# Products of constant ones in TensorE's waits, in a kernel of two attention layers and two Fourier layers

## The chip, the cores and the metric

The kernel runs on one core of one Trainium2 chip. The metric is the device time of that core in microseconds (us), lower is better. A core has TensorE (PE: matrix products into PSUM), VectorE (DVE), ScalarE (ACT) and GpSimd (POOL), and SyncE (SP), whose queue issues the transfers (DMA). Each engine works through its own list of instructions in order; an instruction waits until the semaphores that it names have the counts it asks for.

## The reference

Four sublayers are applied to x (2048 rows of 512 values), each on a layer norm of x and added to x:

```
x = x + A(layernorm(x)); x = x + B(layernorm(x)); x = x + A(layernorm(x)); x = x + B(layernorm(x))

A: q, k, v = x@wq, x@wk, x@wv in 32 heads of 16, four segments of 512 rows
   for each segment: p = softmax(q k^T / 4 + causal mask); a_dot = p v
      a_mem = phi(q) M / (phi(q) z + 1e-6);  o = g a_mem + (1 - g) a_dot
      M += phi(k)^T v;  z += sum phi(k)
   out = o @ wo
B: a = x @ dft_hid_re^T;  b = x @ dft_hid_im^T;  y = dft_seq_re @ a - dft_seq_im @ b
```

## The kernel before, in words

**Products.** Most products of float32 operands are made from float16 pairs (a high and a low half): three products of 128x128 by 128x512 for each block of 128 in the sum (`mm3`, lines 348 to 350). So TensorE's usual instruction is a weight load (LDWEIGHTS) of 128x128 and a product with 512 columns. The scores of the attention are products of 48 or 50 rows, two at a time on the two halves of the rows; the products with v have 32 output rows.

**Generators.** Each part of the work is a generator: `s_p` makes q and k of a segment and of a group of eight heads, `s_x` the scores whose row maxima VectorE takes, `s_st` the transposed scores whose exponentials ScalarE takes, `s_av` the products with v, `s_o` the output projection, `s_ab` and `s_f` the two transforms of B, and `t_...` the steps of other engines that follow a product. A generator yields what its next step needs: the engine, the tiles it reads, and the buffers it will take (`need`, lines 335 and 336).

**PSUM.** The eight banks of PSUM are the tiles `b`, one pool that `take` and `close` hand out by kind: `pj`, `av`, `dft`, `sx`, `st`, `ss`. A product in a bank must wait until the engine that read the bank's last contents is done.

**Where things stand in time.** Up to some 200 us the inputs and weights are loaded and split, and the first segment's attention runs alone. After that the Fourier products of B fill TensorE between the attention's steps, and from some 1480 us on little but Fourier products is left.

## Time and profile before

| | |
|---|---|
| three runs | 1747.06, 1746.74, 1741.66 us; median 1746.74 |
| the profiled execution | 1747.35 us, of which 1745.6 us is the span from the first to the last instruction |
| mean clock granted to TensorE | 0.971 of full speed |
| busy share | PE 96%, DVE 63%, ACT 50%, POOL 43% |

The profile gives for each group of instructions when it began, how long it took, what it wrote and read, how many there were (x), and in brackets how long its engine had been idle just before, with what ended the idle time. A product's record is longer (381 ns in the mean for 128x512) than the step from one start to the next, since a product begins while the last one drains; so a busy TensorE in the page is not one at its peak. "PEclk" is the clock that was granted to TensorE, 1.00 or 0.50 in one slice, as a mean over the stretch.

### The profile page before, as it was taken

How to read it: one execution, taken by the hardware profiler on the slowest of the kernel's cores; microseconds unless marked ns; L12 is line 12 of the kernel's file. 1: busy time of each engine (PE TensorE's matmuls, PEld its weight loads, DVE VectorE, ACT ScalarE, POOL GpSimd, SP SyncE). 2: the span in 40 equal slices, each digit the busy share in tenths (PEclk: the TensorE clock that was granted, in tenths of full speed). 3: DMA queues.
4: the chain of work that ended last, by engine and by line, in shares of the span. 5: the costliest groups of instructions: out<-in, count | busy, mean ns of one | idle time of the engine just before them, and what ended most of it. 6: DMA issues, size and time to landing. Idle time of an engine off the chain costs nothing.

```text
span 1745.6 us, 32094 instructions
## 1 busy us (share of the span) xinstructions
PE 1674.4 (96%) x10998; PEld 730.6 (42%) x10998; DVE 1094.4 (63%) x3525; ACT 870.9 (50%) x1481; POOL 746.2 (43%) x1284
## 2 busy tenths in 40 slices
PE   6888899998999999999999999999999999999999
PEld 3333344443344443444535344443444443344444
DVE  7885856787675967654578676566675856443221
ACT  5597467555548365644366755464446334412000
POOL 4466355555546264633244644444535334312000
PEclk9788999999999999999989999999999999999999
DMA  8537445554247443334845654354444342131423
GB/s 194 165 102 205 109 113 156 150 145 128 77 125 212 139 130 107 108 105 135 223 139 189 188 164 121 74 138 132 113 120 122 94 110 85 56 121 23 136 85 118
DMA packets 217076, 225.00 MB, mean 129 GB/s; under 512 B 112968, under 2 KB 135496, under 8 KB 216912
## 3 DMA queue, kind: packets, MB, share of 16 engines
q1 hardware_dynamic: 216912, 222.95, 45.6%
q8 instruction: 86, 1.41, 0.3%
q14 instruction: 78, 0.64, 0.1%
HBM read 137.40 MB, written 61.87 MB: 114 GB/s over the span
## 4 chain that ended last, share of the span: by engine, by line
PE 80%; DVE 7%; issue 4%; DMA 3%; ACT 3%; POOL 2%; SPq 1%; DVEq 0%; POOLq 0%; ACTq 0%
PE b L258 80%; DVE junk L258 3%; ACT w L258 3%; POOL w L258 2%; DMA w<-w 1%; SPq L258 1%; DVE w L258 1%; DVE y L258 1%; DVE mx L258 1%; DMA x<-y 0%; DMA w<-in_x_dram 0%; DMA y<-in_wv_dram 0%; DVE bst L258 0%; DMA w<-x 0%; DVE cgm L258 0%
## 5 line engine op out<-in xcount | busy, mean ns | idle before, releaser
L258 PEld LDWEIGHTS <-w 128*128 128x128 f16 x4992 | 466.2, 98 | 636.9 <-issue 121.5
L258 PE MATMUL b<-w,w 128*128 128x512 f16 x3072 | 709.9, 381 | 4.2 <-POOL w L258 1.4
L258 ACT ACTIVATE w<-b,fac 128x512 f32<-128x512 f32 (+1 forms) x728 | 417.6, 653 | 196.1 <-PE b L258 191.8
L258 DVE CUSTOM_DVE_ANT_0 junk<-b,cmask 128x128 bf16<-128x128 f32 (+3 forms) x1024 | 437.1, 485 | 70.9 <-PE b L258 70.1
L258 POOL TENSOR_TENSOR w<-w,w 128x512 f16<-128x512 f32 (+1 forms) x260 | 309.2, 1193 | 239.1 <-ACT w L258 204.7
L258 POOL TENSOR_SCALAR_AFFINE_SELECT w<-w 128x128 f32<-128x128 f32 (+2 forms) x704 | 236.7, 348 | 272.6 <-ACT w L258 268.1
L258 DVE SCALAR_TENSOR_TENSOR y<-b,fyu,y 128x512 f32<-128x512 f32 x200 | 149.1, 745 | 210.7 <-PE b L258 209.8
L258 PE MATMUL b<-g,w 128*128 128x512 f16 x768 | 191.1, 394 | 6.7 <-POOL w L258 3.0
L258 ACT ACTIVATE w<-w,csc 128x512 f16<-128x512 f32 (+1 forms) x256 | 179.5, 721 | 25.2 <-DVE csc L258 20.3
L258 PE MATMUL b<-w,vt 128*32 128x512 f32 (+3 forms) x2048 | 181.5, 469 | 6.9 <-POOL w L258 4.7
L258 PE MATMUL b<-wd,w 128*128 128x512 f16 x768 | 182.1, 385 | 4.6 <-DMA w<-w 4.3
L258 ACT ACTIVATE w<-b 128x512 f16<-128x512 f32 x128 | 76.4, 599 | 218.0 <-PE b L258 210.6
L258 DVE SCALAR_TENSOR_TENSOR w<-b,w 128x512 f16<-128x512 f32 x128 | 87.9, 688 | 150.2 <-ACT w L258 149.2
L258 PE MATMUL b<-kst,qst 48*128 48x128 f16 (+3 forms) x1024 | 125.0, 309 | 10.9 <-DVE mx L258 5.0
L258 PE MATMUL b<-qst,kst 50*128 50x512 f16 (+3 forms) x1024 | 119.5, 308 | 10.4 <-DVE mx L258 3.8
L258 ACT ACTIVATE w<-w 128x512 f16<-128x512 f32 (+1 forms) x144 | 90.6, 632 | 58.1 <-DVE w L258 55.9
L258 PEld LDWEIGHTS b<-w,vt 128*32 128x32 f32 x2048 | 56.7, 113 | 95.8 <-issue 52.2
L258 PE MATMUL b<-w,g 128*128 128x128 f16 x1536 | 94.4, 219 | 0.4 <-ACT w L258 0.2
L258 PEld LDWEIGHTS <-g 128*128 128x128 f16 x1536 | 87.8, 98 | 13.9 <-issue 9.1
L258 DVE STREAM_TRANSPOSE w<-b 128x512 f32<-128x512 f32 x112 | 76.4, 699 | 22.1 <-PE b L258 13.7
L258 PE MATMUL b<-wo,w 128*128 128x512 f16 x384 | 89.3, 381 | 0.0
L258 PEld LDWEIGHTS <-kst 50*128 50x128 f16 x1024 | 37.5, 95 | 120.8 <-issue 109.5
(99 smaller groups left out, 1017.8 us busy)
## 6 DMA issues: line engine op xcount, KB each, us to landing
w<-in_cs_dram SPq DMA_DIRECT2D x128, 256.0 KB, 3.6
cc<-w SPq DMA_DIRECT2D x128, 256.0 KB, 2.5
w<-cc SPq DMA_DIRECT2D x128, 256.0 KB, 3.3
w<-w SPq DMA_DIRECT2D x96, 256.0 KB, 3.2
d<-w SPq DMA_DIRECT2D x128, 128.0 KB, 2.5
w<-in_x_dram SPq DMA_DIRECT2D x32, 256.0 KB, 3.2
qst<-d SPq DMA_DIRECT2D x64, 128.0 KB, 3.2
kst<-d SPq DMA_DIRECT2D x64, 128.0 KB, 2.8
```

The source lines that it names most:

```text
L258: r = f(*args, **kw)
```

## The change

Before TensorE's next step is taken, a new function `t_warm` looks at the planned time `at` at which that step can begin, less 200 ns. If TensorE would be idle for at least 220 ns until then, if the products of the last 3413 ns by the plan have under 6500 columns, and if a bank of PSUM of kind `dft` is free at least 430 ns before, then products of the constant tile `onesb` (128x128 ones in bfloat16, there before) with itself, repeated to 512 columns, go to TensorE into that bank, each counted as 215 ns, until the time is up or 6500 columns are reached. Nobody reads the bank's contents. They bypass `Plan.op`, and the books on the bank are put back, so that the plan doesn't see them, and the next step that takes a bank takes that one. Two lines in `op` and the helper `lately` keep the list of columns that the function looks at.

```diff
+WARM, IDLE, SPARE = 6500, 220.0, 200.0
...
+    def lately(self, t):
+
+        return sum(c * max(0.0, min(e, t) - max(b, t - TICK)) / (e - b) for b, e, c in self.work)
...
             self.cols[int((t + c) / TICK)] = self.cols.get(int((t + c) / TICK), 0) + cols
+            self.work.append((t, t + c, cols))
+            while self.work[0][1] < t - 3 * TICK:
+                self.work.popleft()
...
+    def t_warm(at):
+        now, at = pl.free["T"], at - SPARE
+        if "CM" not in done or at - now < IDLE or pl.lately(at) >= WARM:
+            return
+        r = pl.slots_free(("dft",))
+        if r is None or r > at - 430:
+            return
+        now = max(now, r)
...
+        p = ps("dft")
+        while now + 215 < at and pl.lately(at) < WARM:
+            T.real.matmul(p, onesb, onesb.unsqueeze(1).to_broadcast([128, 4, 128]), start=True, stop=True)
+            pl.work.append((now, now + 215, 512))
+            now += 215
...
+        if best[1][0][0] == "T":
+            t_warm(best[0])
         best[1][0] = next(best[1][1], None)
```

The lists of DVE, ACT, POOL and SP are the same as before. TensorE's list has the same instructions in the same order, and 241 products of ones (each with its weight load) between them, in 39 groups. By the place in the profile of before at which the next instruction begins (us), with the number of products:

| Place | Products put in ahead of it |
|---|---|
| 9.47, 15.34, 16.55 | 37, 23, 4 |
| 47.50 to 51.19 | 1, 4, 2, 4, 8, 13 |
| 76.9 and 154.5 | 1 and 2 |
| 113.1 to 134.0 | 2, 2, 3, 3, 4 |
| 140.22 to 143.32 | 15, 7, 5, 1 |
| 185.75, 185.91, 190.56 | 16, 12, 18 |
| 409.4 to 434.8 | 3, 2, 2, 1, 2 |
| 518.9 and 560.06 | 1 and 6 |
| 684.56, 822.46, 838.32 | 4, 14, 3 |
| 890.2 to 891.6 | 2, 4, 2 |
| 976.2, 986.1, 1445.1 | 3, 2, 3 |

The first place is on PE at some 186 us, at the end of an output projection (`b<-wo,w` ends just ahead), where three pairs of scores (`kst,qst`: `qst` is loaded, `kst` streams) stand ahead of the first transform of B (`wd`). Before:

```order
L258 LDWEIGHTS qst_106
L258 MATMUL b_2791<-kst_104,qst_106 128x384
L258 LDWEIGHTS qst_106
L258 MATMUL b_2792<-kst_104,qst_106 128x384
L258 LDWEIGHTS qst_106
L258 MATMUL b_2801<-kst_104,qst_106 128x384
L258 LDWEIGHTS qst_106
L258 MATMUL b_2802<-kst_104,qst_106 128x384
L258 LDWEIGHTS w_2662
L258 MATMUL b_2811<-wd,w_2662 128x512
```

and in the changed kernel, where `L1180` is the line of the new products and L268 is the helper's line that was L258:

```order
L1180 LDWEIGHTS onesb
L1180 MATMUL b_2952<-onesb 128x512
...
L268 LDWEIGHTS qst_106
L268 MATMUL b_2969<-kst_104,qst_106 128x384
...
L1180 LDWEIGHTS onesb
L1180 MATMUL b_2979<-onesb 128x512
...
L268 LDWEIGHTS qst_106
L268 MATMUL b_2992<-kst_104,qst_106 128x384
...
L1180 MATMUL b_3002<-onesb 128x512
...
L268 MATMUL b_3021<-wd,w_2823 128x512
```

The second and the third pair of scores now stand behind 16 and 12 products of ones, and the transform behind 18 more.

The second place is on PE at 838 us, where the projection of a new segment (`g` holds the transposed, normed rows) follows the products of the Fourier transform along the rows (`b<-w,w`). Before:

```order
L258 MATMUL b_11034<-w_10449,w_10965 128x512
L258 LDWEIGHTS w_8329
L258 MATMUL b_11053<-g_10803,w_8329 128x512
L258 LDWEIGHTS w_8329
L258 MATMUL b_11053<-g_10803,w_8329 128x512
```

and in the changed kernel, with the semaphores that each waits for (DMAHW: transfers; PE: TensorE's own count):

```order
L268 MATMUL b_11288<-w_10688,w_11219 128x512
L1180 LDWEIGHTS onesb
L1180 MATMUL b_11307<-onesb 128x512
...
L268 LDWEIGHTS w_8563 [waits DMAHW5_49,DMAHW7_49,DMAHW3_49,DMAHW0_49]
L268 MATMUL b_11311<-g_11042,w_8563 128x512 [waits PE_49]
```

Three products of ones stand ahead of the weight load that waits for transfers, and the first product into the bank that held them names TensorE's own count: it waits until the last of them has ended. So it is behind every group whose bank the next step takes; ahead of the products with v (`w,vt`), which go on in a bank of their own, there is no such wait. In the whole list 139 rows wait for that count, 118 before.

## The prediction

> **What bounds the kernel now.** I read the page's slices and chain first.

> ```profile
> DVE  7885856787675967654578676566675856443221
> PEclk9788999999999999999989999999999999999999
> PE 80%; DVE 7%; issue 4%; DMA 3%; ACT 3%; POOL 2%; SPq 1%; DVEq 0%; POOLq 0%; ACTq 0%
> L258 PE MATMUL b<-w,w 128*128 128x512 f16 x3072 | 709.9, 381 | 4.2 <-POOL w L258 1.4
> ```

> TensorE carries 80% of the chain, so after the first 200 us what TensorE saves or loses moves the end one for one, while in slices two to four (44 to 175 us) the clock is lowest, and VectorE is busy to eight tenths in two of them. The clock is what the change works on. Its pieces, from the table by stretches (time, TensorE's busy time and records, clock):

> ```profile
> core 0: us, PE busy (x), PEclk, DMA share, GB/s
> 50.16:60.40 10.24, 6.73 (x26) 0.50 0.91 269
> 121.84:125.25 3.41, 3.16 (x15) 0.50 0.24 45
> 142.32:149.15 6.83, 6.13 (x20) 0.50 0.96 340
> 190.11:196.93 6.82, 6.37 (x16) 0.50 0.32 66
> 411.97:415.39 3.42, 3.42 (x21) 0.50 0.77 149
> 432.45:435.86 3.41, 2.17 (x20) 1.00 0.41 77
> 435.87:439.28 3.41, 3.27 (x10) 0.50 0.50 66
> 558.75:562.16 3.41, 1.89 (x19) 1.00 0.97 230
> 562.16:565.57 3.41, 2.80 (x15) 0.50 0.60 121
> 685.04:691.87 6.83, 6.63 (x26) 0.50 0.00 0
> 821.57:824.99 3.42, 1.29 (x6) 1.00 0.66 119
> 824.99:828.40 3.41, 3.41 (x10) 0.50 0.61 142
> 838.64:842.05 3.41, 3.41 (x10) 0.50 0.00 0
> 893.25:896.66 3.41, 3.41 (x20) 0.50 0.28 97
> 1658.32:1701.96 43.64, 43.64 (x204) 1.00 0.25 85
> ```

> The clock goes by slices of 3.41 us: a thin slice (821.57: six records; 558.75; 432.45) is followed by one at half speed. From the last row a product costs 43.64 / 204 = 0.214 us at full clock, so 16 fit in a slice, and twice that, 0.43, at half. A full slice at half clock loses 3.41 / 2 = 1.71 us of TensorE's work.

> The other side is where TensorE waits, from its timeline (start, time, instructions, idle just before):

> ```profile
> 9.47 0.59 PE L258 MATMUL b<-amax,ones 128*128 128x2 f32 x2 [9.47 <-DVE amax L258]
> 15.34 0.58 PE L258 MATMUL b<-amax,ones 128*128 128x2 f32 x2 [5.28 <-DVE amax L258]
> 16.55 4.81 PE L258 MATMUL b<-g,w 128*128 128x512 f16 x15 [0.63 <-DMA g<-w]
> 22.52 0.38 PE L258 MATMUL b<-amax,ones 128*128 128x1 f32 x2 [1.16 <-DVE amax L258]
> ...
> 47.50 2.88 PE L258 MATMUL b<-kst,qst 48*128 48x384 f16 x9
> ...
> 51.19 1.01 PE L258 MATMUL b<-g,w 128*128 128x512 f16 x2
> 55.22 0.61 PE L258 MATMUL b<-g,w 128*128 128x512 f16 x1 [3.01 <-POOL w L258]
> 56.10 0.40 PE L258 MATMUL b<-identf,mx 128*32 128x128 f32 x1 [0.28 <-DVE mx L258]
> ...
> 140.22 2.39 PE L258 MATMUL b<-qst,kst 50*128 50x512 f16 x8 [2.46 <-DMA qst<-mhl]
> 143.32 2.74 PE L258 MATMUL b<-g,w 128*128 128x512 f16 x6 [0.70 <-DMA w<-w]
> ...
> 185.57 0.66 PE L258 MATMUL b<-kst,qst 48*128 48x384 f16 x6
> 190.56 1.46 PE L258 MATMUL b<-wd,w 128*128 128x512 f16 x3 [4.32 <-DMA w<-w]
> ...
> 562.77 1.92 PE L258 MATMUL b<-w,vt 128*32 128x256 f32 x12 [2.09 <-POOL w L258]
> ...
> 822.46 0.61 PE L258 MATMUL b<-w,w 128*128 128x512 f16 x2 [0.75 <-ACT w L258]
> 824.45 11.79 PE L258 MATMUL b<-w,w 128*128 128x512 f16 x46 [1.38 <-POOL w L258]
> 838.32 4.45 PE L258 MATMUL b<-g,w 128*128 128x512 f16 x12 [2.08 <-DMA g<-w]
> ...
> 889.72 2.51 PE L258 MATMUL b<-kst,qst 48*128 48x384 f16 x8
> ...
> 1445.11 0.28 PE L258 MATMUL b<-identf,mx 128*32 128x128 f32 x1 [1.00 <-DVE mx L258]
> ```

> The products of ones were placed by planned waits. Some stand at a wait that the trace has (838.32, 1445.11), some a few products ahead of one (562.77), and some where there is none: the 16 and 12 within the six scores of 185.57.

> **What the products cost.** Nothing is removed or moved, no transfer and no queue of another engine is touched; so each group costs its number times 0.214 less what waits at or just behind it. By places:

> Start, 64 products, 13.7 us against 9.47 + 5.28 + 0.63 of waits. They can begin only when VectorE has written the ones:

> ```profile
> 1.50 0.17 DVE L258 MEMSET onesb<- 128x128 bf16 x1
> ```

> That is after 1.7 us, and the first run at half clock: ten at 0.43 and 27 at 0.214 end at 11.8, 2.3 late. VectorE's next maxima hang on that product, so the next two groups only follow, and the first projection begins at some 18.8 instead of 16.55, now at full clock: 15 x 0.214 = 3.2 against the 4.81 shown, so it ends at 22.0. The next product waits for VectorE until 22.52 anyway. Cost 0; if that cover fails, up to 1.

> 47 to 51 us, 32 products, 6.85. From 47.3 TensorE has some 2.1 us of its own work (twelve records, the scores in pairs, with the changes of shape) up to the product at 55.22: it gets there at 56.25, 1.03 late, of which the 0.28 ahead of 56.10 takes back some. Cost 0.75.

> 77 and 154 us: three products, 0.64. 113 to 134 us: 14 products; VectorE is busy in eight tenths of that slice and TensorE waits for it between the scores, so I count two as bare, 0.4.

> 137 to 143 us: 28 products, 6.0 us at full clock, less 2.46 and 0.70 of waits, and less some 1.1 that the eight scores save at full clock: 1.7 (they stood at half, 2.39).

> 185 to 190 us: 46 products, 9.84 less 4.32: 5.5, the largest item. The wait at 190.56 ends with a transfer that starts from work done before 185, so it doesn't move.

> 409 to 435 us: ten products among scores that wait for ScalarE's and VectorE's evictions; two bare, 0.4. 519 us: 0.2. 560 us: six, 1.28, within the 2.09 that ends at 562.77: 0. 684 us: four, 0.3 bare. 822 us: 14, 3.0 less 0.75 and 1.38: 0.9. 838 us: three, 0.64 under 2.08: 0. 890 us: eight at half clock, 3.4, less some 0.6 of pauses in the eight scores, whose row is all but busy: 2.8. 976 and 986 us: five bare, 1.1. 1445 us: 0.64 under 1.00: 0.

> Sum: 0.75 + 0.64 + 0.4 + 1.7 + 5.5 + 0.4 + 0.2 + 0.3 + 0.9 + 2.8 + 1.1 = 14.7 us.

> The wait for TensorE's own count is new. No row shows it alone. Its lower end is 0, where a wait follows anyway; its upper end is a product that can't begin while the last one drains, 0.381 - 0.214 = 0.17 us. Some 24 groups have no wait to hide it; at the middle, 0.1 (neither row is nearer), 2.4 us; at the upper end 4.1. **Cost: 17.1 us.**

> **What the clock gives back.** For each slice that the products fill, half the busy time of the slice that was at half speed behind it, where TensorE bounds:
> 50.16: from 56.1 to 60.4 only, 4.1 / 2 = 2.0. 121.84: 1.5. 142.32: its last 5.8 us, 2.9. 190.11: 3.2. 411.97: its second part alone, 1.3, as the first waits for ScalarE. 562.16: 1.4. 685.04: two slices, 3.3, but only the first products of that group fall into the slice before; even odds, 1.6. 824.99: 1.7. 838.64: 1.7. 893.25: 1.7. **Gain: 19.0 us.** The thin slices to which little or nothing is added stay (432.45 gets two products).

> Net: 17.1 - 19.0 = -1.9. The profiled execution took 1747.35, so 1745.4; that execution lies 0.6 above the median of the runs, so **1744.8 us**.

> [...] In the trace TensorE is idle for 1.24 us in all between 432.45 and 435.86 (3.41 less 2.17), and half clock follows. [...]

> **Rivals.** Within 0.3% is what a measurement of this kernel can't tell from no change (1741.5 to 1752.0); my forecast lies there, with a chance of 0.47 and that as its own range.

> Faster, 0.33: the own-count waits hide in the changes of shape (-2.4), the even-odds slices at 685 come back whole (+1.7), and the groups at 185 and 890 meet waits that the changed clock moves under them (some -3 of their 8.3). That is -1.9 - 2.4 - 1.7 - 3 = -9, 1738. For it: the slices after 200 us are full (3.41 of 3.41 busy), so nothing but TensorE can take their gain. Against it: the gains before 200 us (9.6) lie where VectorE is busy too.

> Slower, 0.13: the overrun decides. Its place is the six scores at 185.57 and the eight at 889.72, where the products stand ahead of work that doesn't wait, and the group at 137, which at half clock costs 28 x 0.43 = 12 instead of 6. If the clock isn't up by 137, the sum gets +6, and with a gain of 14.5 (the slices of 142 and 685 missed) it is 23.1 - 14.5 = +8.6: 1755. It decides once the gain is under 12 at the cost above.

> Slower, 0.05: only waits of a whole slice halve the clock, so that the ones between shorter waits buy nothing: 2.0 + 3.2 are won for 17.1, +11.9: 1758.6. Against it stand the rows of 432.45 and 558.75.

> Not what it says, 0.02: the clock doesn't count products that read the same constants; nothing is won, and what stands at half clock costs double (28 at 137, 46 at 185): 17.1 + 6.0 + some 8 = +31, 1778.

> **Chances and range.** Faster 0.33, within 0.47, slower 0.13 + 0.05 + 0.02 = 0.20. The range takes the faster case to 1736 (which leaves out some 0.06 below) and the slower ones to 1754 (0.13 above): 1736 to 1754.

> **What would show it.** In the changed profile: clock 1.00 in the stretches behind 56, at 143 to 149, 191 to 197, 562, 825 and 839 us, mean clock from 0.971 to some 0.985; the product at 55.22 about a microsecond late, the transform of 190.56 some 5 us later against the end of the output projection; no later start at 22.52 and behind 838. Half clock still there behind the filled slices refutes the gain; the transform on time at 190 refutes the largest cost; a 22.52 that moves shows that the start was not covered.

## The result, and the profile after

The changed kernel takes 1752.4 us, median of six runs (1749.98 to 1755.52), beside 1747.07 (1741.66 to 1748.81) for the kernel before: a ratio of 1.0036, interval 1.0018 to 1.0053. It is slower by 5.3 us where 2 us of gain were forecast. Run again beside the experiments it gave 1.0051 (1.0034 to 1.0068). Single runs of one kernel lie 10 us and more apart, so all comparisons below are of medians, with the 95% interval of the ratio to the kernel before.

The profiled execution took 1751.29 us, and its page shows a clock that rose and an end that came later all the same:

```profile
span 1749.6 us, 32573 instructions
PE 1707.0 (98%) x11239; PEld 746.3 (43%) x11239; DVE 1093.7 (63%) x3525; ACT 871.0 (50%) x1481; POOL 747.7 (43%) x1284
PEclk9889999999999999999989999999999999999999
PE 79%; DVE 8%; issue 4%; DMA 3%; ACT 3%; POOL 2%; SPq 1%; DVEq 0%; ACTq 0%; POOLq 0%
```

The mean clock is 0.985, to the digit what was forecast (0.971 before), in part by luck: some of the slices it was to come from stayed at half, and others did not, as shown below. The profiled execution of before had a low clock, though: the median over the kernel's runs is 0.974 to 0.975, beside 0.984 to 0.9855 for the changed kernel, so the usual rise is 0.010 to 0.011 and not 0.014. The pieces at half clock, added up from the two traces, fell from 103.5 to 53.6 us. The stretches that answer to those of before (time, TensorE's busy time and records, then the other engines, clock, DMA share, GB/s):

```profile
56.20:60.40 4.20, 4.14 (x30) 1.80 (x29) 3.29 (x16) 1.09 (x3) 1.72 (x2) 1.00 0.59 214
117.67:121.08 3.41, 1.14 (x6) 0.29 (x6) 2.74 (x13) 1.66 (x4) 2.95 (x6) 1.00 0.02 7
121.08:127.91 6.83, 6.38 (x28) 1.10 (x29) 5.49 (x21) 6.77 (x13) 4.21 (x10) 0.50 0.41 87
141.56:148.39 6.83, 6.66 (x32) 2.48 (x30) 3.74 (x10) 6.80 (x12) 4.48 (x11) 1.00 0.93 334
192.76:196.17 3.41, 3.41 (x16) 1.47 (x15) 0.62 (x5) 1.44 (x2) 1.15 (x1) 1.00 0.00 0
564.80:568.21 3.41, 3.41 (x65) 2.68 (x64) 2.65 (x21) 1.17 (x2) 1.77 (x3) 1.00 0.90 276
680.86:684.27 3.41, 2.80 (x12) 0.68 (x11) 3.41 (x12) 2.77 (x5) 0.88 (x3) 1.00 0.81 298
684.27:691.10 6.83, 6.69 (x26) 1.60 (x27) 5.86 (x23) 3.08 (x6) 2.75 (x8) 0.50 0.00 0
824.23:827.64 3.41, 3.35 (x17) 1.55 (x16) 0.75 (x2) 3.35 (x6) 3.26 (x5) 1.00 0.48 118
834.47:837.88 3.41, 1.01 (x5) 0.28 (x3) 1.91 (x3) 0.00 (x0) 0.00 (x0) 1.00 1.07 226
837.88:841.29 3.41, 3.17 (x8) 1.20 (x9) 0.03 (x1) 0.00 (x0) 0.00 (x0) 0.50 0.05 18
885.67:889.08 3.41, 2.02 (x8) 0.66 (x8) 3.41 (x15) 2.63 (x5) 1.91 (x4) 1.00 0.48 156
889.08:899.32 10.24, 10.03 (x38) 2.13 (x35) 7.15 (x27) 6.62 (x11) 5.07 (x9) 0.50 0.35 113
```

Full clock came where it was forecast behind 56, 142, 192, 562 and 824 us. It did not come at 121, 684, 838 and 889 us: the row of 834.47 holds five records, and the next slice is at half; the row of 885.67 holds eight, and the three slices behind it are.

TensorE's timeline of the same execution at the groups (start, time, instructions, idle just before):

```profile
1.73 9.77 PE L1180 MATMUL b<-onesb 128*128 128x512 bf16 x37 [1.73 <-DVE onesb L268]
11.55 0.38 PE L268 MATMUL b<-amax,ones 128*128 128x2 f32 x2
...
17.22 1.02 PE L1180 MATMUL b<-onesb 128*128 128x512 bf16 x4
18.30 3.40 PE L268 MATMUL b<-g,w 128*128 128x512 f16 x15
22.18 0.38 PE L268 MATMUL b<-amax,ones 128*128 128x1 f32 x2 [0.47 <-DVE amax L268]
...
53.57 2.98 PE L1180 MATMUL b<-onesb 128*128 128x512 bf16 x13
56.60 0.81 PE L268 MATMUL b<-g,w 128*128 128x512 f16 x3
...
184.81 0.34 PE L268 MATMUL b<-kst,qst 48*128 48x384 f16 x2
185.08 3.63 PE L1180 MATMUL b<-onesb 128*128 128x512 bf16 x16
188.76 0.34 PE L268 MATMUL b<-kst,qst 48*128 48x384 f16 x2
189.03 2.76 PE L1180 MATMUL b<-onesb 128*128 128x512 bf16 x12
191.85 0.34 PE L268 MATMUL b<-kst,qst 48*128 48x384 f16 x2
192.13 4.06 PE L1180 MATMUL b<-onesb 128*128 128x512 bf16 x18
196.24 0.81 PE L268 MATMUL b<-wd,w 128*128 128x512 f16 x3
...
684.84 1.89 PE L1180 MATMUL b<-onesb 128*128 128x512 bf16 x4
...
834.67 0.81 PE L1180 MATMUL b<-onesb 128*128 128x512 bf16 x3
838.12 4.30 PE L268 MATMUL b<-g,w 128*128 128x512 f16 x12 [2.64 <-issue]
...
891.37 1.89 PE L1180 MATMUL b<-onesb 128*128 128x512 bf16 x4
```

At 192.13 the last 18 products begin after the whole wait of before (4.32 us up to 190.56) is over: the 28 ahead of them have used it up, and the transform that began at 190.56 begins at 196.24. At 684.84 and 891.37 four products take 1.89 us, at half clock, where 0.86 would be the price at full.

Since TensorE's real products are the same in the same order, each can be matched between two traces. The table gives how much later (+) or earlier it is reached, step by step, than in the trace of before (places by before's time, us; one execution each). "Without the 28" and "late 40" are experiments below.

| Place | forecast, own-count waits apart | changed | changed again | without the 28 | late 40 |
|---|---|---|---|---|---|
| start to 41 | 0 | -1.4 | -1.9 | -0.8 | +1.1 |
| 41 to 60 | -1.25 | +0.6 | +4.0 | +0.7 | 0.0 |
| 60 to 182 | -1.7 | +0.1 | -1.4 | -0.3 | -1.7 |
| 182 to 202 | +2.3 | +3.5 | +3.5 | -2.75 | +0.1 |
| 202 to 440 | -0.9 | -2.7 | -0.7 | -3.7 | -2.7 |
| 516 to 705 | -2.5 | +0.3 | -1.0 | -0.5 | -0.8 |
| 817 to 852 | -2.5 | -0.7 | -0.5 | -0.65 | -2.8 |
| 852 to 920 | +1.1 | +3.3 | +4.2 | +2.0 | +0.1 |
| 955 to 1005 | +1.1 | -1.4 | -1.4 | -0.9 | -2.0 |
| 1005 to 1300 | 0 | +2.1 | +2.5 | +0.75 | -0.6 |

The same kernel profiled twice differs by 3.4 us at 41 to 60 us alone, so a single row says little unless it repeats; 182 to 202 and 852 to 920 do. The last row has no products in it, and a run with products in the first 17 us alone shows +2.8 there too: so it is not the price of products there; what it comes from stays open. At 955 to 980 us all four traces are earlier than that of before by 1.6 us or more, and so is the one with products in the first 17 us alone (2.7): the trace of before had a slice at half clock at 964.93 that theirs lack.

### The profile page after: what moved, and what is told of

Same layout as the page of the kernel before. It is cut to its first block, busy times and chain, and to the rows that moved or that the text cites. A ratio compares the mean times of both kernels' runs of the same rounds, so it can differ in the third digit from the quotient of the medians.

```text
span 1749.6 us, 32573 instructions
## 1 busy us (share of the span) xinstructions
PE 1707.0 (98%) x11239; PEld 746.3 (43%) x11239; DVE 1093.7 (63%) x3525; ACT 871.0 (50%) x1481; POOL 747.7 (43%) x1284
## 4 chain that ended last, share of the span: by engine, by line
PE 79%; DVE 8%; issue 4%; DMA 3%; ACT 3%; POOL 2%; SPq 1%; DVEq 0%; ACTq 0%; POOLq 0%
PE b L268 77%; DVE junk L268 3%; ACT w L268 2%; PE b L1180 2%; DMA w<-w 2%; DVE w L268 1%; SPq L268 1%; POOL w L268 1%; DMA w<-in_x_dram 1%; DVE mx L268 1%; DVE y L268 1%; DVE bst L268 0%; DMA y<-in_wv_dram 0%; DVE cam L268 0%; DVE mv L268 0%
## 5 line engine op out<-in xcount | busy, mean ns | idle before, releaser
L268 PEld LDWEIGHTS <-w 128*128 128x128 f16 x4992 | 463.9, 98 | 614.9 <-issue 110.1
L268 PE MATMUL b<-w,w 128*128 128x512 f16 x3072 | 707.3, 380 | 2.1 <-DVE w L268 0.9
L268 ACT ACTIVATE w<-b,fac 128x512 f32<-128x512 f32 (+1 forms) x728 | 417.8, 653 | 196.0 <-PE b L268 191.7
L268 DVE CUSTOM_DVE_ANT_0 junk<-b,cmask 128x128 bf16<-128x128 f32 (+3 forms) x1024 | 437.6, 486 | 74.3 <-PE b L268 73.6
L268 POOL TENSOR_TENSOR w<-w,w 128x512 f16<-128x512 f32 (+1 forms) x260 | 309.2, 1194 | 247.6 <-ACT w L268 212.7
L268 POOL TENSOR_SCALAR_AFFINE_SELECT w<-w 128x128 f32<-128x128 f32 (+2 forms) x704 | 238.1, 349 | 277.0 <-ACT w L268 272.1
L268 DVE SCALAR_TENSOR_TENSOR y<-b,fyu,y 128x512 f32<-128x512 f32 x200 | 149.2, 746 | 211.1 <-PE b L268 210.4
L268 ACT ACTIVATE w<-w,csc 128x512 f16<-128x512 f32 (+1 forms) x256 | 179.5, 721 | 27.2 <-DVE csc L268 22.4
L268 PE MATMUL b<-g,w 128*128 128x512 f16 x768 | 184.6, 384 | 3.1 <-issue 2.6
L268 ACT ACTIVATE w<-b 128x512 f16<-128x512 f32 x128 | 76.4, 600 | 217.9 <-PE b L268 208.4
L268 DVE SCALAR_TENSOR_TENSOR w<-b,w 128x512 f16<-128x512 f32 x128 | 88.0, 688 | 151.2 <-ACT w L268 150.2
L268 PE MATMUL b<-wd,w 128*128 128x512 f16 x768 | 179.2, 381 | 0.2
L268 PE MATMUL b<-w,vt 128*32 128x512 f32 (+3 forms) x2048 | 173.6, 456 | 3.0 <-POOL w L268 2.1
L268 PE MATMUL b<-kst,qst 48*128 48x128 f16 (+3 forms) x1024 | 122.3, 306 | 10.0 <-DVE mx L268 4.9
L268 PE MATMUL b<-qst,kst 50*128 50x512 f16 (+3 forms) x1024 | 116.5, 304 | 8.6 <-DVE mx L268 5.3
L268 ACT ACTIVATE w<-w 128x512 f16<-128x512 f32 (+1 forms) x144 | 90.7, 632 | 60.3 <-DVE w L268 57.8
L268 PE MATMUL b<-w,g 128*128 128x128 f16 x1536 | 94.4, 219 | 0.6 <-DMA w<-w 0.2
L268 PEld LDWEIGHTS <-g 128*128 128x128 f16 x1536 | 87.6, 98 | 13.6 <-issue 8.1
L268 PEld LDWEIGHTS b<-w,vt 128*32 128x32 f32 x2048 | 54.4, 111 | 89.9 <-issue 52.6
L268 DVE STREAM_TRANSPOSE w<-b 128x512 f32<-128x512 f32 x112 | 76.5, 700 | 22.7 <-PE b L268 17.6
L268 PE MATMUL b<-wo,w 128*128 128x512 f16 x384 | 88.7, 379 | 0.1
L268 PEld LDWEIGHTS <-kst 50*128 50x128 f16 x1024 | 37.5, 95 | 117.5 <-issue 112.6
```

What stands on the lines that cost most here:

```text
L268: r = f(*args, **kw)
```

## The experiments

All experiments number the 39 groups in the order of the program (0 to 2 at the start, 3 to 8 at 47 to 51 us, 15 to 18 at 140, 20 and 21 the 16 and 12 within the six scores, 22 the 18 ahead of 190.56, 28 at 519, 29 at 560, 30 at 684, 31 and 32 at 822 and 838, 33 to 35 at 890, 36 and 37 at 976 and 986, 38 at 1445). A group that is left out is still counted in the plan's books, so that the others stay as they are; the order of all real instructions is that of the changed kernel. The edit that all share:

```diff
+        i = nth[0]
+        nth[0] += 1
+        if KEEP is not None and i not in KEEP:
+            n = 0
+        if GIVE:
+            n = GIVE.get(i, n)
+        if not n:
+            return
```

The theories: A, the products that stand where no wait is cost their length and one wait is paid for twice; B, every group costs more than its length (the wait for TensorE's own count, the change of shape); C, what the clock gives does not reach the end, since other engines bound; D, the loss is the group at 890; P, what a group gains depends on where the slices of 3.41 us fall (near 835 us one begins at 838.64 in the trace of before, at 834.47 in that of the changed kernel and at 831.19 in that of the late 40); S, the parts add up.

**Without the groups that stand where no wait is (199 products).**

```diff
+KEEP = {0, 1, 2, 3, 4, 5, 6, 7, 8, 9, 10, 11, 12, 13, 14, 15, 16, 17, 18, 19, 22, 23, 24, 25, 26, 27, 29, 30, 31, 32, 38}
```

> 199 of the 241 products: without those that the trace of before shows bare (16 and 12 at 185, eight at 890, one at 519, three at 976, two at 986). Theory A, overrun: the clock gives back what was forecast and the loss is products ahead of work that does not wait; then the wait at 190.56 covers its 18 products, 6.0 + 3.4 + 1.3 us go, and the kernel is some 5 us faster than before (1740 to 1744). Theory B, the products cost beyond their length everywhere (the wait for TensorE's own count, changes of shape): at most a quarter of the loss goes, 1749 to 1752. Theory C, the clock's gain does not reach the end: within 2 us of before.

Measured 0.9963 (0.9949 to 0.9978), 1740.87 us. Leaving out 42 of the 241 products turns the loss into a gain, as A put it. But by the forecast's own terms the 199 should have been some 10 us faster than before (-1.9, less 5.5 and 2.4 for the 42 and 0.8 for their own-count waits); they are 5 to 6 faster. So products without a wait are not the whole of the error.

**Those 42 alone.**

```diff
+KEEP = {33, 34, 35, 36, 37, 20, 21, 28}
```

> The other 42 products alone (16 and 12 at 185, one at 519, eight at 890, three at 976, two at 986). Theory A: 9.0 us of products of which the 28 at 185 also fill the wait at 190.56 (6.0 less 4.32, and 3.2 back from the clock), so 3 to 5 us slower than before, 1750 to 1752. Theory B: the same and 0.2 to 0.3 for each of eight groups, 1752 to 1755. Theory C: 1.7 + 3.4 + 1.3 without anything back, 6.4 slower, 1753.5.

Measured 0.9979 (0.9965 to 0.9994), 1742.56 us: not slower at all, a miss for A, B and C as they were put (1750 to 1755). Alone, the 28 stand against a wait of 4.32 us that nothing else fills, and 182 to 202 us took 0.6 us less than before. The mean clock, by the median of the runs, is 0.9775 beside 0.974, some 6 us of TensorE's work in 1745 (an estimate: the difference times the span). That half clock fell from 103.5 to 85.2 us in the trace shows little by itself: the run with 22 products at 986 us, below, had 84.5. The same products cost or gain by what stands beside them.

**All 241, one column each.** It does the weight loads and the waits of the change, but 1 of 512 columns.

```diff
-            T.real.matmul(p, onesb, onesb.unsqueeze(1).to_broadcast([128, 4, 128]), start=True, stop=True)
+            T.real.matmul(p[:, :1], onesb, onesb[:, :1], start=True, stop=True)
```

> All 241 products with one column instead of 512 (the weight load and the waits stay, the time in the array is gone). Theory A: 0 to 3 us slower than before, and the clock as before (0.971). Theory B: the waits for TensorE's own count and the changes of shape are most of the loss, 4 to 8 us slower. Theory C: within 1 us of before.

Measured 1.0012 (0.9999 to 1.0025), 1749.68 us. So loads, shapes and own-count waits of all groups come to 2.1 us together, 4.4 by the upper end (the plain medians lie 3.9 apart). The clock hides nothing here: its median over the runs is 0.974 in both kernels. It also has a slice with many records (the stretches at 185 us of this run, columns as above):

```profile
184.77:188.18 3.41, 1.98 (x50) 1.55 (x46) 3.31 (x8) 1.32 (x2) 1.41 (x2) 1.00 0.72 183
188.19:191.60 3.41, 2.20 (x6) 0.52 (x7) 3.01 (x14) 0.58 (x2) 1.66 (x2) 0.50 0.44 88
```

Fifty records in the first slice, 1.98 us of it busy, and half clock (0.50) behind it: the number of products alone did not bring full clock.

**The next step goes on in the same bank tile.** Without a new tile there is no wait for TensorE's own count; 117 rows have one, where 139 had.

```diff
+        t = self.spare.pop(b, None) if ar["prefix"] == "b" else None
+        if t is None or list(shape) != [128, 512]:
+            t = ar["pool"].tile(list(shape), dt, name=f"{ar['prefix']}{b}", bufs=1)
```

> All 241 products at full width, but the next step that takes their bank goes on in the same tile where it has the same shape, so that its first product does not wait for TensorE's own count (117 rows wait for it, 139 in the changed kernel). Theory A: 1 to 3 us under the changed kernel, 1749.5 to 1751.5. Theory B: 4 to 8 under it, 1744 to 1748. Theory C: as the changed kernel within 1 us.

Measured 1.0020 (1.0005 to 1.0035), 1749.91 us, against 1.0036 and 1.0051 with the waits: 3 to 5 us better at face value, with intervals that overlap.

**The same without the 42.**

```diff
+KEEP = {0, 1, 2, 3, 4, 5, 6, 7, 8, 9, 10, 11, 12, 13, 14, 15, 16, 17, 18, 19, 22, 23, 24, 25, 26, 27, 29, 30, 31, 32, 38}
```

> The 199 products of the run rest, and the next step goes on in the bank's same tile, so that it does not wait for TensorE's own count. Theory A: 0 to 2 us under rest, 0.9955 to 0.9965 of before. Theory B: 3 to 5 us under rest, 0.9935 to 0.995.

Measured 0.9970 (0.9957 to 0.9982), 1738.62 us, beside 0.9963 with the waits: no gain. And with all 241 products but without the waits the kernel is still slower than before (1.0020 above). B is not what made the loss, though it may have a part in it.

**The changed kernel again**, with no edit, beside the next two.

> The changed kernel once more, beside the kernels of this call. All theories: 1.003 to 1.005 times the kernel before, as measured.

Measured 1.0051 (1.0034 to 1.0068), 1754.08 us.

**Without the 28 within the six scores (213 products).**

```diff
+KEEP = {0, 1, 2, 3, 4, 5, 6, 7, 8, 9, 10, 11, 12, 13, 14, 15, 16, 17, 18, 19, 22, 23, 24, 25, 26, 27, 28, 29, 30, 31, 32, 33, 34, 35, 36, 37, 38}
```

> 213 products: without the 16 and 12 ahead of the second and third pair of scores at 185 alone. Theory A, paid twice: the 28 and the 18 behind them both go for the one wait of 4.32 us at 190.56, so without the 28 some 5 to 6 us of the changed kernel's loss go and it stands at 0.998 to 1.001 of before. Theory B, each product costs a little everywhere: 28 of 241, 1.002 to 1.004. Theory D, the eight at 890 are the most of it: 1.002 to 1.004.

Measured 0.9995 (0.9979 to 1.0012), 1742.45 us, 0.0056 below the changed kernel. TensorE's timeline of this run:

```profile
185.25 0.66 PE L270 MATMUL b<-kst,qst 48*128 48x384 f16 x6
185.84 4.06 PE L1197 MATMUL b<-onesb 128*128 128x512 bf16 x18
190.43 0.82 PE L270 MATMUL b<-wd,w 128*128 128x512 f16 x3 [0.53 <-DMA w<-w]
```

The 18 fill the wait and leave 0.53 us of it; the transform begins at 190.43, on time (190.56 before), and its first three products take 0.82 us, where they took 1.46 at half clock before.

**Without the 14 at 519, 890, 976 and 986 (227 products).**

```diff
+KEEP = {0, 1, 2, 3, 4, 5, 6, 7, 8, 9, 10, 11, 12, 13, 14, 15, 16, 17, 18, 19, 20, 21, 22, 23, 24, 25, 26, 27, 29, 30, 31, 32, 38}
```

> 227 products: without the eight at 890, three at 976, two at 986 and one at 519. Theory A: 1.5 to 3 us of the changed kernel's loss go, 1.001 to 1.0035. Theory B: 14 of 241, nothing that can be seen, 1.003 to 1.004. Theory D: 5 us go, 0.9995 to 1.001.

Measured 1.0015 (1.0001 to 1.0028), 1746.37 us, 0.0036 below. D has a part in it, not the whole.

**The 46 at 185 to 190 alone.**

```diff
+KEEP = {20, 21, 22}
```

> Only the 46 products at 185 to 190, nothing else. Theory A, paid twice: 9.84 us of products less the one wait of 4.32, with 3.2 back from the half clock behind it: 2 to 3.5 us slower than before, 1.001 to 1.002; in the profile the distance from the end of the output projection to the products at 202 us grows by 2.5 to 3.5 us. Theory B, the loss is spread over all groups: within 1 us of before, 0.9995 to 1.0005. Theory D, the loss is at 890: as theory B.

Measured 1.0005 (0.9989 to 1.0022), 1745.26 us. By the trace 182 to 202 us took 3.49 us longer than before, the very figure of the changed kernel and what A said; but A's time, 1.001 to 1.002, did not come at face value, and with an uncertainty of 3 us the median does not tell the theories apart.

**The price: 22 products at 986, where there is no wait, and no others.**

```diff
+KEEP = set()
+GIVE = {37: 22}
```

> Only the group at 986, where no wait is, with 22 products instead of two, to measure the price of a bare product. Theory A: 22 x 0.214 = 4.7 us and 0.2 for the wait for TensorE's own count, 4.9 us slower, 1.0028. Theory B, that a product costs more than its step: 6 us or more, 1.0035. Theory C, that TensorE's time there does not reach the end: under 2 us.

Measured 1.0030 (1.0016 to 1.0044): medians 4.4 us apart. TensorE's timeline of this run:

```profile
979.83 2.76 PE L270 MATMUL b<-w,w 128*128 128x512 f16 x12
982.43 4.91 PE L1197 MATMUL b<-onesb 128*128 128x512 bf16 x22
987.39 2.10 PE L270 MATMUL b<-w,w 128*128 128x512 f16 x9
```

From 982.43 to 987.39 is 4.96 us, 22 x 0.225, and product by product the stretch from 980 to 1005 us is later than before by as much. A bare product cost its length here, and the end moved by all of it, within the interval.

**The 54 behind 400 us alone.**

```diff
+KEEP = {23, 24, 25, 26, 27, 28, 29, 30, 31, 32, 33, 34, 35, 36, 37, 38}
```

> Only the 54 products after 400 us (16 groups). Theory A: their cost of 6.1 us and 1 us of waits for the own count against a gain of 9.4 by the forecast's terms: 2 us faster, 0.9985 to 0.9995. Theory P, the free-running slices: the small groups of two to six do not bring their slice over the bound in most executions, so half of the gain: 1 to 3 us slower, 1.0005 to 1.002.

Measured 0.9998 (0.9981 to 1.0015), 1744.85 us: between the theories, and undecided.

**The 199 cut to the waits.** 186 products: groups in long waits raised, those that overran shortened.

```diff
+KEEP = {0, 1, 2, 3, 4, 5, 6, 7, 8, 9, 10, 11, 12, 13, 14, 15, 16, 17, 18, 19, 22, 23, 24, 25, 26, 27, 29, 30, 31, 32, 38}
+GIVE = {8: 8, 15: 12, 16: 5, 17: 0, 18: 0, 29: 9, 31: 11, 32: 9, 38: 0}
```

> 186 products, as many as the waits of before hold: rest, with the groups at 55, 137 to 143 and 822 cut (13 to 8, 28 to 17, 14 to 11), those at 560 and 838 raised to nine each, none at 1445. Theory A: 1 to 3 us under rest (0.9963 and 0.997 with and without the own count), so 0.994 to 0.996. Theory P: the raised groups at 560 and 838 bring their slices over the bound at every phase, another 1 us. Theory C: 0.996 to 0.998, as rest.

Measured 0.9971 (0.9959 to 0.9983), 1739.39 us: faster than both kernels, and no better than the uncut 199. Fitting the counts more closely bought nothing that can be measured; A's 0.994 to 0.996 and P's further 1 us did not come.

**The groups up to 191 us, with the 28 (187 products).**

```diff
+KEEP = {0, 1, 2, 3, 4, 5, 6, 7, 8, 9, 10, 11, 12, 13, 14, 15, 16, 17, 18, 19, 20, 21, 22}
```

> The groups up to 191 us alone, 187 products with the 28 within the six scores; none of the 54 behind 400 us. Theory S (each group's cost and gain stand by themselves and add up): the changed kernel measured 1.0051 and the late 54 alone 0.9998, so 1.005. Theory P (what a group gains depends on where the slice boundaries fall when it is reached, so parts don't add): no set figure; the half-clock pieces behind 400 us are those of the kernel before (some 50 us), and the time at 182 to 202 us is +3.5.

Measured 1.0019 (1.0002 to 1.0036), 1749.06 us; 182 to 202 us took 3.49 us longer, as expected. S's 1.005 did not come. Nor did P's sign: half clock behind 400 us was 27.3 us in this trace and 41.0 in that of before, though both kernels have the same instructions there. One execution differs from the next by that much.

**And without the 28 (159 products).**

```diff
+KEEP = {0, 1, 2, 3, 4, 5, 6, 7, 8, 9, 10, 11, 12, 13, 14, 15, 16, 17, 18, 19, 22}
```

> The same without the 28 products within the six scores: 159 products up to 191 us. Theory S: the kernel without the 28 measured 0.9995 with the late 54 at 0.9998, so 0.9997 here; the difference to the run with the 28 is 28 x 0.214 = 6.0 us of 1745, 0.0034, if a wait pays only once, and more (0.0056, as between the changed kernel and the one without the 28) if the 28 also push later work.

Measured 0.9983 (0.9969 to 0.9996), 1743.13 us. Against the run above the 28 cost 0.0036, 6.3 us, beside 6.0 for their length and 6.24 by the table (3.49 + 2.75). S expected 0.9997 and is off by 2.4 us, about the interval.

**The late groups without the 14 (40 products).**

```diff
+KEEP = {32, 38, 23, 24, 25, 26, 27, 29, 30, 31}
```

> Only 40 products behind 400 us, those at 409 to 435, 560, 684, 822, 838 and 1445 us; the 14 at 519, 890, 976 and 986 us left out as well. Theory S: the kernel that leaves the 14 out of the change measured 1.0015 against 1.0051, so 0.9998 - 0.0036 = 0.996; the products' own length would give only 14 x 0.214 = 3.0 us, 0.0017, so 0.998.

Measured 0.9967 (0.9953 to 0.9981), 1740.07 us: six times fewer products than the change, and as large a gain as any other version here (its own time beside 1745.21); it lies between S's 0.996 and the 0.998 of the length alone. TensorE's timeline and the stretches at 833 us of this run:

```profile
830.29 0.81 PE L1197 MATMUL b<-onesb 128*128 128x512 bf16 x3
833.23 2.75 PE L270 MATMUL b<-g,w 128*128 128x512 f16 x12 [2.13 <-issue]
```

```profile
831.19:834.60 3.41, 1.37 (x7) 0.69 (x8) 1.92 (x3) 0.00 (x0) 0.00 (x0) 1.00 0.69 146
834.61:838.02 3.41, 3.41 (x19) 1.52 (x18) 1.49 (x6) 1.86 (x3) 0.00 (x0) 1.00 0.00 0
```

The same three products, a wait of the same kind, and the projection at full clock: 12 products take 2.75 us instead of 4.30. The slice here began at 831.19, after the three, and took in the projection's first products (seven records); in the changed kernel it began at 834.47, with the three, and ended before the projection (five).

**The first 64 alone.**

```diff
+KEEP = {0, 1, 2}
```

> Only the 64 products of the first 17 us. In the traces with them the product at 41 us is 3.5 to 4 us earlier than before, and then up to 4 us of it are lost by 60 us, where other products stand. If the start's gain lasts where no products follow: 0.998 (3.5 of 1745). If VectorE, which is busy in eight tenths of the first 200 us, takes it back: 1.000.

Measured 0.9987 (0.9974 to 1.0000), 1742.6 us: 2.3 us, between the two answers. The 3.5 to 4 us that were expected count from the first product, which is some 2 to 3 us late in these traces; against the start of the span the lead at 41 us is 0.9 here (1.4 and 1.9 in the changed kernel's two). At 202 us nothing of it is left (+1.0).

## Why the prediction was wrong

**The step that failed is what the clock gives back.** It put ten slices at 19.0 us, "for each slice that the products fill". In the changed kernel's trace four of them were at half clock all the same: 121.84 (1.5), 685.04 (1.6), 838.64 (1.7) and 893.25 (1.7), together 6.5 us. All four have half clock in the second trace of the changed kernel too, and the three rows of the table that hold the last three of them are 6.8 and 6.6 us worse than forecast in the two traces. With 12.5 instead of 19.0 the sum is 17.1 - 12.5 = +4.6, where +5.3 was measured (medians) and +3.9 in the trace.

That these figures lie so close is in part luck. The changed kernel's trace also lacks slices at half clock that the forecast had not counted, 418.80 and 964.93 among them, up to 1.7 us each, and 2.1 us were lost between 1005 and 1300 us, where no product was put in. The runs with one part alone, below, give another division of the same term: if the costs stood as forecast, the early groups gained 6.5 of 9.6 us, the late 40 gained 7.4 of 7.7, and the 14 none of 1.7, so about 14 instead of 19.0. The term was too large by both; at which places is told only for the changed kernel's own traces.

Where the products fell can be told. In the slices ahead of the four TensorE was busy for 1.14 us (117.67), 2.80 (680.86), 1.01 (834.47) and 2.02 (885.67) of 3.41. Only the slice of 834.47 held products of ones, three in five records (0.81 us). The four meant for 680.86 begin at 684.84, in the next slice, which is itself at half; the eight meant for 885.67 begin at 889.84, in the slices behind it, at half as well; 117.67 held none. In the slices ahead of the five that came to full clock TensorE was busy for 2.82 to 3.41 us, with 15 products of ones (52.79), 14 (138.15), 15 (189.35), six (561.39) and 14 (820.82).

Busy time alone does not tell: in the trace of the late 40 the slice of 831.19 had 1.37 us, and full clock follows, while 2.80 at 680.86 were followed by half. What does, no run shows; that the products "fill" a slice was the author's estimate. Behind the groups of 13 to 18 products at 53.57, 137.32, 192.13 and 821.07 the clock was full. Behind smaller ones it was either: full behind the six at 560, half behind the three at 834.67, the four at 684.84 and the eight at 890, full behind the very three of 834.67 where the slices lay elsewhere (830.29 in the late 40). The plan's window, "the last 3413 ns" ahead of a step, does not lie where the traces' slices lie, and neither did the slices I counted on: I took those of one trace of before as fixed.

**The cost sum stood in the main, and where it was called largest.** In four parts, without the own-count waits, and as measured by the runs that hold or leave out each part (ratio times 1745):

| Part | forecast | measured |
|---|---|---|
| up to 191 us, 159 products | 3.5 - 9.6 = -6.1 | -3.0 (-5.4 to -0.7) |
| behind 400 us, 40 products | 1.6 - 7.7 = -6.1 | -5.8 (-8.2 to -3.3) |
| the 28 within the six scores | +5.5 | +6.3 (by the early pair), +9.8 (by the whole) |
| the 14 at 519, 890, 976, 986 | 4.1 - 1.7 = +2.4 | +5.4 (late pair), +6.3 (whole) |
| sum | -4.3, with 2.4 of own-count waits -1.9 | +2.9 to +7.3 |

The 28 cost what their length says, since one wait of 4.32 us was paid for twice: "transform of 190.56 some 5 us later" came as 6.4 (from the first score to the transform 11.43 us, 4.99 before). The 14 are 3 us or more worse: their 1.7 of gain at 893 did not come, and the two bare ones at 986 cost 0.65 us in the trace, of which 0.43 is their length; the rest is open. The early groups gave half of the net that was forecast. Half clock before 200 us was 27.3 and 34.1 us in the changed kernel's traces. In four kernels without a product there it was 61.4, 61.4, 54.6 and 41.0 (before, late, late 40, and 22 at 986). Half the difference, some 3 to 17 us, is an estimate of what TensorE had back; the early groups' run shows 6.5 if their cost stood. With that spread the shortfall needs no further reason. The prediction had named one, VectorE, busy in the same slices, and given it no term; no run took VectorE's work away, so whether it had a part stays open.

**The own-count wait**, 2.4 in the sum with 0 to 4.1: the one-column run puts it, with the loads, at 2.1 and below 4.4 net; the pair of 199 shows none, the pair of 241 shows 3 to 5 with intervals that overlap. It doesn't explain the loss: without these waits the change still measured 1.0020 (1.0005 to 1.0035).

**What was right.** The start was covered: the first projection at 18.30 (18.8 forecast), the product of 22.52 at 22.18, so no later. The projection of 55.22 is 1.38 us late (about 1 forecast), and by 60 us, with the clock at 1.00 from 56.20 on, that is won back (-1.4 + 0.6 by the table). Clock 1.00 came at five of the six places named, not behind 839.

**The rivals.** The nearest is the overrun: its two places, 185.57 and 889.72, are those whose removal makes the kernel faster, and its point, "once the gain is under 12", is near the 12.5 to 14 that came. It did not come as it was put: the reason it gave, the clock still down at 137, did not happen (the slice of 138.15 is at 1.00, and 15 products of ones take 3.41 us from 137.32 on). The faster one did not come: the groups at 185 and 890 met no wait that moved under them (182 to 202 and 852 to 920 us are later in both traces), and the even odds at 685 were lost. Waits of a whole slice alone did not decide: half clock follows a slice that was idle for 2.40 us in all (834.47: 3.41 less 1.01), and one idle for 0.61 (680.86). And products of constants were followed by full clock: the slice ahead of 141.56 held 14 of them in 18 records (2.81 of its 3.35 us of busy time), the one ahead of 192.76 held 15 in 17 (3.08 of 3.35), and both rows are at 1.00.

**What stays open.** The parts sum to +2.9 to +7.3 and the change measured +5.3 to +9; intervals of 2 to 3 us a part hide whether they add up exactly. That the same 42 products cost 13 to 15 us on top of the others (0.9963 against 1.0036 and 1.0051) and gain 3.7 alone is explained in part by the wait that only one of two groups can use (6.2 us). The phase of the slices is argued from the traces for the rest; no run sets the phase, and none separates the two.

## What to carry to other kernels

Where TensorE bounds, filling a wait to keep the clock up was worth, by estimate, at most 1.7 us here for each slice saved (half of 3.41) and cost 0.22 us for each product that the wait did not cover (4.96 us for 22 at 986); so put them at single long waits, once each, and count the wait as used up by the first group. Forty products at six places gained as much here (0.33%) as 199 at thirty-one. A mean clock or a busy share that rises proves nothing of the time: this change met its forecast clock and lost 5 us.

## What the runs showed of the hardware

The clock's slices of 3.41 us began at another place in each of three traces: near 835 us from the first instruction one begins at 838.64 (before), 834.47 (changed) and 831.19 (late 40), which lie 4.17 and 3.28 apart. One kernel's time at half clock differs from execution to execution (53.6 and 61.7 us in all in the two traces of the changed kernel, mean clock 0.985 and 0.983). The kernel's time varies by 10 us in 1745 and goes along with the clock: among 32 runs of the kernel before, those with a lower clock tend to be slower (correlation -0.6).

Full clock followed five slices of the changed kernel's trace with 2.82 to 3.41 us of TensorE's busy time, and one with 1.37 in that of the late 40 (831.19). Half clock followed four of the changed kernel's with 1.01 to 2.80, and one of 1.98 with fifty records, most of them of one column (184.77 of the one-column run). Neither busy time nor the number of records alone tells which follows, and no run shows what does. A slice with 15 products of ones in 17 records was followed by full clock (192.76).
